# Four of a kernel's first loads on ScalarE's DMA queue, issued after a memset by GpSimd

## The chip, the cores and the metric

The kernel runs on one core of a Trainium2 chip. The metric is device microseconds for one execution, as the median of several runs; less is better. The core has five engines with a queue of instructions each: TensorE (PE), VectorE (DVE), ScalarE (ACT), GpSimd (POOL) and SyncE (SP). SP and ScalarE can also issue transfers between the chip's memory and SBUF. Each of the two has a ring of its own on the same 16 DMA engines; in the rows q1 is SP's ring and q10 is ScalarE's.

## The reference

A gated linear attention (4 batches, 8 heads, 768 steps, head size 48), and a soft mixture of 8 experts with 4 slots each on its output:

```python
f = 1.0 / (1.0 + np.exp(-f_logit))
for t in range(S):
    state = f[:, :, t, :, None] * state + np.einsum('bhd,bhe->bhde', k[:, :, t], v[:, :, t])
    y[:, :, t] = np.einsum('bhd,bhde->bhe', q[:, :, t], state)
...
logits = x @ phi                       # x: (3072, 384), the attention's output
d = softmax of logits over the rows; slot_input = d.T @ x
slot_out[e] = np.maximum(slot_input[e] @ w1[e], 0.0) @ w2[e]
return (softmax of logits over the slots) @ slot_out
```

All inputs and outputs are float32.

## The kernel before, in words

The attention is done in chunks of 128 steps, as 12 blocks u; a block holds half of the heads and batches in tiles of 128 partitions by 1024 columns for f, k and q, and 768 for v. Blocks 0 and 1 are worked off in two halves h of 512 columns, so that the first work can begin after a small load. A step is named as in `load.k.0.1`: the load of k, block 0, half 1. One half load is 128 rows of 2 KB, 256 KB.

For a block, ScalarE takes exp and ln of the gate logits (`d_exp` L267, `d_ln` L271), VectorE runs a prefix sum over them (`d_scan` L274), ScalarE takes exp of it with both signs (`d_g` L277, `d_p` L280), and k and q are multiplied by these (`d_k` L284, `d_q` L288). TensorE transposes k (`kt` L302), forms the scores (L331), which VectorE masks (`s_mask` L336), and then the products with v: `kv` (L348) for the running state, `intra` (L384) and `inter` (L378) for the output. `warm` (L240) is a matmul on constants at the start. The logits, the slot inputs and the two expert layers follow; their weights w1 and w2 are loaded by SP all the while and used in the last third.

The order of all steps is written out by hand in the list `ORDER`, and `keep_order` binds the instructions of each engine to it. `load` (L260) puts a transfer on ScalarE's queue if its name stands in `BY_ACT`, and on SP's otherwise. f has two buffers, and so have k and q.

At the start ScalarE's queue issues k.0.0 and q.0.0, SP's queue f.0.0, f.0.1, f.1.1, q.0.1, f.1.0, k.0.1, v.0 and then the next blocks. GpSimd clears `esum` (`c_esum`, L234: 128x24, named check in the rows), waits for `ones` from VectorE, and makes the mask and the identity.

Of the kernel before, what the change touches and what calls it, by code (L numbers as in the profile page):

```python
# [42 lines left out]
load_phi d_q.1.1 d_ln.2.0 kt.1.0 intra.0.0 d_pend.1 state_t.0 intra.0.1 kt_copy.1 d_scan.2.0 d_ln.2.1 load.f.3 y_copy.0 d_scan.2.1 scores.1.0 d_g.2.0
d_k.2.0 scores.1.1 x_tr.0 s_mask.1.0 d_g.2.1 d_p.2.0 load.q.2 kv.1 load_w2.4 intra.1.0 s_mask.1.1 d_p.2.1 d_k.2.1 d_exp.3 state_t.1 d_ln.3 d_pend.2
hint.Pool d_q.2 kt.2.1 d_scan.3 kt.2.0 intra.1.1 kt_copy.2 x_copy.0 load.v.2 y_copy.1 d_g.3 scores.2.0 scores.2.1 load.q.3 s_mask.2.0 load.k.3 x_tr.1
d_p.3 s_mask.2.1 inter.2 kv.2 load.f.4 intra.2.0 x_copy.1 d_k.3 intra.2.1 kt.3.1 load.k.4 kt.3.0 d_exp.4 load.v.3 d_ln.4 state_t.2 kt_copy.3 d_q.3
load.q.4 d_pend.3 c_lg.0 scores.3.0 d_scan.4 y_copy.2 c_lt.0 load.f.5 scores.3.1 s_mask.3.0 c_max.0 d_g.4 inter.3 d_p.4 kv.3 d_k.4 intra.3.0 c_exp.0
load_w1.4 s_mask.3.1 load_w1.2 hint.SP load.k.5 intra.3.1 c_tr.0.1 load.v.4 c_tr.0.0 d_exp.5 d_q.4 d_pend.4 d_ln.5 kt.4.0 state_t.3 load.f.6 load.q.5
c_copy.0 kt.4.1 x_tr.2 state_s.2 y_copy.3 scores.4.0 kt_copy.4 scores.4.1 d_scan.5 state_s.3 s_mask.4.0 x_copy.2 d_g.5 s_mask.4.1 inter.4 d_exp.6
c_pin.0 c_join.0 d_p.5 d_k.5 d_q.5 c_same.1 kv.4 intra.4.0 d_ln.6 load.v.5 kt.5.1 load_w1.10 x_tr.3 kt.5.0 intra.4.1 x_copy.3 state_t.4 kt_copy.5  # L50
c_lg.1 d_pend.5 load.k.6 load.f.7 y_copy.4 d_scan.6 c_al.0 d_g.6 c_max.1 d_p.6 scores.5.0 scores.5.1 s_mask.5.0 load.q.6 inter.5 c_exp.1 c_lt.1 d_k.6
s_mask.5.1 c_same.3 intra.5.0 load_w1.6 intra.5.1 d_pend.6 load_w2.1 d_q.6 load.v.6 d_exp.7 c_al.1 kt.6.0 load.k.7 kt.6.1 y_copy.5 c_tr.1.0 c_tr.1.1
c_copy.1 kv.5 load.q.7 load.f.8 d_ln.7 kt_copy.6 state_t.5 state_s.4 load_w2.5 x_tr.4 scores.6.0 load.v.7 d_scan.7 s_mask.6.0 scores.6.1 load_w1.3
x_copy.4 inter.6 c_pin.1 d_g.7 intra.6.0 s_mask.6.1 d_k.7 d_exp.8 d_p.7 kv.6 c_join.1 load.q.8 x_tr.5 state_s.5 kt.7.1 d_q.7 state_t.6 kt.7.0
intra.6.1 d_ln.8 load.k.8 load.f.9 x_copy.5 c_sum.1 d_pend.7 c_lg.2 kt_copy.7 d_scan.8 y_copy.6 d_g.8 d_k.8 scores.7.0 scores.7.1 c_max.2 s_mask.7.0
load_w1.1 load.v.8 c_exp.2 c_lt.2 inter.7 load_w1.8 c_tr.2.0 d_p.8 c_tr.2.1 s_mask.7.1 d_exp.9 d_ln.9 intra.7.0 c_copy.2 kv.7 kt.8.1 x_tr.6 load.q.9
state_t.7 kt.8.0 intra.7.1 d_q.8 d_pend.8 load.k.9 x_copy.6 c_soft.0.0 c_sum.0 c_same.0 c_pin.2 c_al.2 d_scan.9 kt_copy.8 c_join.2 state_s.6 y_copy.7
c_soft.1.0 load.f.10 scores.8.1 d_g.9 scores.8.0 c_sum.2 load_w1.0 x_tr.7 d_k.9 d_p.9 x_copy.7 d_pend.9 s_mask.8.0 inter.8 intra.8.0 c_lg.3 d_exp.10
s_mask.8.1 d_ln.10 d_q.9 state_s.7 load_w1.13 kt.9.0 c_lt.3 c_max.3 kt.9.1 load.k.10 kv.8 d_scan.10 load.f.11 load.v.9 c_exp.3 load.q.10 load_w1.12
kt_copy.9 intra.8.1 state_t.8 load.v.10 y_copy.8 c_tr.3.1 d_g.10 c_tr.3.0 d_k.10 scores.9.1 c_al.3 scores.9.0 c_copy.3 state_s.0 x_tr.8 s_mask.9.0  # L60
d_p.10 hint.ACT d_exp.11 load.k.11 s_mask.9.1 c_soft.2.0 load_w1.14 inter.9 x_copy.8 d_ln.11 d_q.10 c_sum.3 d_pend.10 intra.9.0 kv.9 intra.9.1
state_t.9 d_scan.11 state_s.8 load.q.11 load.v.11 c_pin.3 scores.10.1 scores.10.0 y_copy.9 d_g.11 state_s.9 c_join.3 x_tr.9 x_copy.9 s_mask.10.1
d_k.11 inter.10 d_p.11 d_pend.11 s_mask.10.0 c_lg.4 intra.10.0 load_w2.2 intra.10.1 c_max.4 c_exp.4 c_lt.4 d_q.11 c_same.2 load_w1.11 c_tr.4.1
c_tr.4.0 c_copy.4 scores.11.0 y_copy.10 s_mask.11.0 scores.11.1 x_tr.10 c_pin.4 x_copy.10 c_al.4 c_soft.3.0 s_mask.11.1 c_join.4 inter.11 intra.11.0
load_w1.15 load_w2.9 intra.11.1 y_copy.11.0 y_copy.11.1.True end c_lg.5 load_w1.7 flag.0 c_soft.4.0 load_w2.8 x_tr1.11.0 x_tr1.11.1 c_sum.4 c_max.5
c_min.5 c_lt.5 c_exp.5 load_w1.9 load_w1.5 t_max.0 x_copies.11.0 c_tr.5.1 x_copies.11.1 c_tr.5.0 t_max.1 load_w2.10 c_ct.0.0 t_max.2 c_copy.5
load_w2.6 flag.1 c_al.5 c_pre.5 load_w2.14 t_max.3 hint.DVE c_ct.0.1 t_max.4 c_pin.5.0 c_pin.5.1 t_max.5 c_be.5 c_join.5.0 t_psi.0 load_w2.0
c_join.5.1 t_psi.1 load_w2.12 t_psi.2 flag.2 up.0.0.0 up.0.1.0 c_soft.0.1 up.0.0.1 up.0.0.2 load_w2.3 relu.0.0 load_w2.11 up.0.1.1 up.0.1.2 turn.0.0.0
up.1.0.0 turn.0.0.1 relu.0.1 up.1.0.1 down.1.0.0 down.1.0.1 down.0.0.0 down.1.0.2 down.1.0.3 read_flag.Pool down.0.0.1 c_soft.1.1 c_soft.2.1
down.0.0.2 load_w2.16 down.0.0.3 read_flag.ACT up.1.0.2 c_sum.5 up.1.1.0 load_w2.13 c_soft.3.1 relu.1.0 up.1.1.1 turn.0.1.0 t_z.0 turn.1.0.0  # L70
load_w2.15 turn.0.1.1 load_w2.22 up.1.1.2 load_w2.19 down.1.0.4 down.1.0.5 down.1.0.6 turn.1.0.1 down.0.0.4 down.0.0.5 load_w2.7 down.0.0.6 down.0.0.7
c_soft.4.1 down.0.1.0 down.0.1.1 load_w2.17 load_w2.18 relu.1.1 load_w2.21 turn.1.1.0 turn.1.1.1 t_z.1 t_z.2 down.0.1.2 down.1.0.7 down.0.1.3
down.1.1.0 down.0.1.4 down.0.1.5 down.0.1.6 down.0.1.7 down.1.1.1 c_ct.1.0 slot_out.0 slot_out2.0.0 slot_out2.0.1 down.1.1.2 down.1.1.3 c_ct.1.1
combine.0.0 result.0.0.1 result.0.0.3 down.2.0.0 result.0.0.0 combine.0.1 result.0.1.3 down.1.1.4 down.1.1.5 result.0.0.2 down.1.1.6 down.1.1.7
hint.PE down.2.0.1 down.2.0.2 down.2.0.3 load_w2.20 down.2.0.4 result.0.1.2 state_s.1 down.2.0.5 result.0.1.1 load_w2.23 down.2.0.6 result.0.1.0
slot_out.1 slot_out2.1.0 slot_out2.1.1 down.2.0.7 down.2.1.0 down.2.1.1 combine.1.0 down.2.1.2 result.1.0.2 result.1.0.0 down.2.1.3 down.2.1.4
result.1.0.1 down.2.1.5 down.2.1.6 down.2.1.7 combine.1.1 slot_out.2 result.1.0.3 result.1.1.0 result.1.1.1 result.1.1.3 store.0.0 store.0.1
result.1.1.2 slot_out2.2.0 store.1.0 read_flag.PE slot_out2.2.1 combine.2.0 read_flag.DVE result.2.0.0 result.2.0.1 result.2.0.3 store.1.1 combine.2.1
# [898 lines left out]
```

## Time and profile before

| | |
|---|---|
| median of 3 runs | 154.32 us (154.18 to 154.73) |
| the profiled execution | 154.26 us |
| its span, first to last instruction | 152.5 us |
| mean granted TensorE clock | 0.99 |
| TensorE busy | 139.0 us, 91% |
| VectorE busy | 109.2 us, 72% |
| ScalarE busy | 95.2 us, 62% |
| GpSimd busy | 43.7 us, 29% |
| moved by DMA | 53.96 MB, mean 354 GB/s |

The profile is of one execution. Its page lists the busy time of each engine, the chain of work that ended last, and groups of instructions by line. The trace behind it also answers for single stretches: the timeline, the chain in time order, the DMA issues with their time to landing, the packets of each ring, and busy times by window. Times are microseconds from the span's start. SPq and ACTq are the DMA issues of SP and ScalarE. An instruction may start a little before the one ahead of it on its engine has ended. In the rows k, q, f and v all lie in one tile, arena.

### The profile page before, as it was taken

How to read it: one execution, taken by the hardware profiler on the slowest of the kernel's cores; microseconds unless marked ns; L12 is line 12 of the kernel's file. 1: busy time of each engine (PE TensorE's matmuls, PEld its weight loads, DVE VectorE, ACT ScalarE, POOL GpSimd, SP SyncE). 2: the span in 40 equal slices, each digit the busy share in tenths (PEclk: the TensorE clock that was granted, in tenths of full speed). 3: DMA queues.
4: the chain of work that ended last, by engine and by line, in shares of the span. 5: the costliest groups of instructions: out<-in, count | busy, mean ns of one | idle time of the engine just before them, and what ended most of it. 6: DMA issues, size and time to landing. Idle time of an engine off the chain costs nothing.

```text
span 152.5 us, 5621 instructions
## 1 busy us (share of the span) xinstructions
PE 139.0 (91%) x2443; PEld 105.8 (69%) x2443; DVE 109.2 (72%) x155; ACT 95.2 (62%) x160; POOL 43.7 (29%) x50
## 2 busy tenths in 40 slices
...
GB/s 154 333 410 272 292 389 335 275 289 413 401 408 354 360 410 411 404 385 408 312 421 385 385 380 370 401 416 417 408 407 408 410 408 409 247 129 296 258 396 184
DMA packets 14574, 53.96 MB, mean 354 GB/s; under 512 B 1616, under 2 KB 1744, under 8 KB 14544
## 3 DMA queue, kind: packets, MB, share of 16 engines
...
q10 hardware_dynamic: 288, 0.52, 0.9%
q8 instruction: 20, 0.33, 0.8%
q14 instruction: 10, 0.08, 0.2%
...
## 4 chain that ended last, share of the span: by engine, by line
PE 78%; DVE 10%; DMA 4%; ACT 3%; issue 2%; DVEq 0%; SPq 0%; ACTq 0%
PE Y L384 13%; PE T L331 13%; PE Z L616 7%; PE Z L560 7%; PE T L405 6%; PE Y L378 6%; PE T L302 5%; PE T L348 5%; PE T L426 3%; PE Z L641 3%; DVE arena L274 3%; DMA arena<-in_f_dram 2%; DMA out_dram<-wr 2%; PE T L487 2%; DVE arena L336 2%
## 5 line engine op out<-in xcount | busy, mean ns | idle before, releaser
L284 POOL TENSOR_TENSOR arena<-arena 128x1024 f32<-128x1024 f32 (+1 forms) x12 | 25.3, 2111 | 43.4 <-ACT arena L277 37.9
L336 DVE TENSOR_TENSOR arena<-T,mask 128x1024 f32<-128x1024 f32 x24 | 28.3, 1212 | 3.2 <-PE T L331 3.2
L274 DVE TENSOR_TENSOR_SCAN arena<-smask,arena 128x1024 f32<-128x1024 f32 (+1 forms) x15 | 27.8, 1857 | 2.9 <-ACT arena L271 2.2
L331 PEld LDWEIGHTS T<-arena 48*128 48x128 f32 x384 | 22.4, 188 | 4.3 <-issue 2.7
L331 PE MATMUL T<-arena 48*128 48x128 f32 x384 | 24.9, 279 | 0.0
L384 PE MATMUL Y<-arena 128*48 128x128 f32 x368 | 24.5, 275 | 0.0
L384 PEld LDWEIGHTS Y<-arena 128*48 128x48 f32 x368 | 20.1, 123 | 2.4 <-issue 1.7
L288 DVE TENSOR_TENSOR arena<-arena 128x1024 f32<-128x1024 f32 (+1 forms) x14 | 17.1, 1230 | 1.4 <-ACT arena L280 1.3
L394 ACT COPY arena<-Y 112x1024 f32<-112x1024 f32 (+1 forms) x12 | 11.7, 978 | 6.7 <-PE Y L384 4.1
L277 ACT ACTIVATE arena<-arena 128x1024 f32<-128x1024 f32 (+1 forms) x15 | 13.3, 889 | 3.9 <-DVE arena L274 3.6
L662 POOL COPY small<-wr 128x1 f32<-128x1 f32 x1 | 0.2, 189 | 52.6 <-DVE wr L658 52.6
L267 ACT ACTIVATE arena<-arena 128x1024 f32<-128x1024 f32 (+1 forms) x15 | 13.2, 881 | 2.9 <-DMA arena<-in_f_dram 2.9
L271 ACT ACTIVATE arena<-arena 128x1024 f32<-128x1024 f32 (+1 forms) x15 | 13.3, 884 | 0.3
L280 ACT ACTIVATE arena<-arena 128x1024 f32<-128x1024 f32 (+1 forms) x15 | 13.1, 884 | 0.4
L360 POOL TENSOR_TENSOR arena<-arena,check 128x384 f32<-128x384 f32 x8 | 11.5, 1441 | 1.8 <-DVE arena L356 1.8
L408 ACT COPY arena<-T 128x768 f32<-128x768 f32 x11 | 8.7, 795 | 5.1 <-PE T L405 4.5
L302 PE MATMUL T<-ident,arena 112*128 112x112 f32 x80 | 10.5, 266 | 1.4 <-DVE arena L284 1.0
L560 PE MATMUL Z<-wr,lt 128*32 128x512 f32 x96 | 11.1, 595 | 0.4 <-DVE lt L549 0.4
L378 PE MATMUL Y<-arena 48*48 48x128 f32 x304 | 11.1, 274 | 0.0
L405 PE MATMUL T<-ident,arena 112*128 112x112 f32 x88 | 10.7, 264 | 0.3 <-DVE pin L494 0.3
L645 DVE COPY wr<-Z 128x384 f32<-128x384 f32 x12 | 6.0, 552 | 6.9 <-PE Z L641 6.9
L568 DVE TENSOR_TENSOR arena<-Z,emask 128x512 f32<-128x512 f32 x4 | 2.7, 690 | 11.2 <-PE Z L571 11.2
...
## 6 DMA issues: line engine op xcount, KB each, us to landing
...
```

The source lines that it names most:

```text
L271: nc.scalar.activation(x, x, AF.Ln, bias=1.0)
L274: nc.vector.tensor_tensor_scan(cols(R("g"), h), cols(smask, h), cols(R("f", u), h), 0.0, op0=ALU.mult, op1=ALU.add)
L277: nc.scalar.activation(cols(R("f", u), h), cols(R("g"), h), AF.Exp)
L284: (eng or nc.gpsimd).tensor_tensor(x, x, cols(R("f", u), h), op=ALU.mult)
L288: (eng or nc.vector).tensor_tensor(x, x, cols(R("g"), h), op=ALU.mult)
L302: nc.tensor.transpose(ps.T0[:, w, 128 * p : 128 * p + R2], kq[:R2, 4 * w + p], ident[:R2, :R2])
L331: nc.tensor.matmul(TB(u, w)[:, r, 128 * p : 128 * p + 128], kq[rs, 4 * w + p], qq[rs, 4 * w + p], start=True, stop=True)
L336: nc.vector.tensor_tensor(scv[:, w].rearrange("p r a t -> p (r a) t"), TB(u, w).rearrange("p r (a t) -> p (r a) t", t=L), mask.unsqueeze(1 ...
L378: nc.tensor.matmul(y_at(u, p, r, w), st[rs, 4 * w + p], qq[rs, 4 * w + p], start=w == 0 and p < 2, stop=False, skip_group_check=True)
L384: nc.tensor.matmul(y_at(u, p, r, w), vv[:, 4 * w + p, r], scv[:, w, r, p], start=u < 2 and w == 0 and p < 2, stop=w == 1 and p > 1, skip_g ...
L405: nc.tensor.transpose(TX(u)[:, w, 128 * k : 128 * k + R2], yblock(u, w, k), ident[:R2, :R2])
L560: nc.tensor.matmul(upt(j, hf)[32 * qq : 32 * qq + 32], si[:, c], w1u[2 * qq + j, hf][:, c], start=c == 0, stop=c == 2)
```

## The change

`BY_ACT` gets two more entries, so that ScalarE's queue issues k.0.0, q.0.0, q.0.1 and k.0.1, in this order, all ahead of its first `d_exp`. A new step `c_first` lets GpSimd write zeros to the first 256 columns of the place that k.0.0 is loaded to. It comes directly after `c_esum`; the load of k.0.0 has to wait for it, and the loads behind it on ScalarE's queue with it. SP's queue then holds f.0.0, f.0.1, f.1.1, f.1.0, v.0 and the rest. On VectorE and TensorE the order stays as it was; `c_smask` is only written at another place of the list.

```diff
-BY_ACT = (("k", 0, 0), ("q", 0, 0))
+BY_ACT = (("k", 0, 0), ("q", 0, 0), ("q", 0, 1), ("k", 0, 1))
...
 ORDER = """
-c_smask load.f.0.0 c_esum load.f.0.1 load.k.0.0 load.q.0.0 d_exp.0.0 c_ones c_zero warm load.f.1.1 d_ln.0.0 load.q.0.1 load.f.1.0 load.k.0.1 d_exp.0.1
-d_scan.0.0 d_ln.0.1 d_g.0.0 warm d_scan.0.1 c_mask c_ident d_p.0.0 d_g.0.1 warm d_p.0.1 load.v.0 d_exp.1.1 load.k.1 d_pend.0 d_k.0.0 warm d_ln.1.1
+c_esum c_first load.f.0.0 load.f.0.1 load.k.0.0 load.q.0.0 load.q.0.1 load.k.0.1 c_smask d_exp.0.0 c_ones c_zero warm load.f.1.1 d_ln.0.0 load.f.1.0
+d_exp.0.1 d_scan.0.0 d_ln.0.1 d_g.0.0 warm d_scan.0.1 c_mask c_ident d_p.0.0 d_g.0.1 warm d_p.0.1 load.v.0 d_exp.1.1 load.k.1 d_pend.0 d_k.0.0 warm
...
     def c_esum():
         nc.gpsimd.memset(esum, 0.0)
 
+    def c_first():
+
+        nc.gpsimd.memset(cols(R("k", 0), 0)[:, :256], 0.0)
+
...
-    for x, fn in enumerate((c_ones, c_smask, c_ident, c_mask, c_esum, c_zero)):
+    for x, fn in enumerate((c_esum, c_first, c_ones, c_smask, c_ident, c_mask, c_zero)):
```

The rest of `ORDER` is the same list with other line breaks.

## Rows read from the trace of the kernel before

**Rows 1.** The page: TensorE's busy time (part 1), chain by engine (part 4).

```profile
PE 139.0 (91%) x2443; PEld 105.8 (69%) x2443; DVE 109.2 (72%) x155; ACT 95.2 (62%) x160; POOL 43.7 (29%) x50
...
PE 78%; DVE 10%; DMA 4%; ACT 3%; issue 2%; DVEq 0%; SPq 0%; ACTq 0%
```

**Rows 2.** The chain in time order, first 16.5 us: start, duration, what.

```profile
0.81 3.30 DMA arena<-in_f_dram
...
4.20 0.73 ACT arena L267 x2
...
5.58 0.70 ACT arena L267 x2
...
6.96 1.24 DVE arena L274
...
15.09 0.92 PE T L348 x32
```

**Rows 3.** Timeline of VectorE, 8 to 17: start, duration, line, out<-in [idle before].

```profile
9.55 0.69 DVE L288 TENSOR_TENSOR arena<-arena 128x512 f32<-128x512 f32 x1 [0.17 <-ACT arena L280]
10.16 0.68 DVE L284 TENSOR_TENSOR arena<-arena 128x512 f32<-128x512 f32 x1
10.88 2.44 DVE L274 TENSOR_TENSOR_SCAN arena<-smask,arena 128x512 f32<-128x512 f32 x2
```

**Rows 4.** Timeline of all engines: the start, and one later GpSimd memset.

```profile
0.80 0.12 POOL L234 MEMSET check<- 128x24 f32 x1 [0.29 <-POOLq L962]
...
0.81 1.33 SPq L260 DMA_DIRECT2D arena<-in_f_dram  x3
0.83 0.38 ACTq L260 DMA_DIRECT2D arena<-in_k_dram  x1
...
1.25 0.45 ACTq L260 DMA_DIRECT2D arena<-in_q_dram  x1
...
2.18 0.43 SPq L260 DMA_DIRECT2D arena<-in_q_dram  x1
...
2.35 0.29 POOL L231 TENSOR_SCALAR_AFFINE_SELECT mask<-ones 128x128 f32<-128x128 f32 x1 [1.43 <-DVE ones L221]
...
3.13 0.44 SPq L260 DMA_DIRECT2D arena<-in_k_dram  x1
...
4.13 0.33 SPq L260 DMA_DIRECT2D arena<-in_v_dram  x1
...
15.29 0.31 POOL L247 MEMSET emask<- 128x256 f32 x1
```

**Rows 5.** Issue to landing: f.0.0; f.0.1 and f.1.1 (min, max); q.0.1; k.0.1.

```profile
DMA to landing us min/median/max: 3.3/3.3/3.3
...
DMA to landing us min/median/max: 4.3/5.2/6.1
...
DMA to landing us min/median/max: 6.3/6.3/6.3
...
DMA to landing us min/median/max: 6.7/6.7/6.7
```

**Rows 6.** Packets, MB, share of engines by ring: first 2.1 to 2.6, then 2.6 to 3.0.

```profile
q1 hardware_dynamic: 36, 0.07, 42.1%
q10 hardware_dynamic: 12, 0.02, 15.9%
...
q10 hardware_dynamic: 41, 0.08, 54.3%
q1 hardware_dynamic: 33, 0.07, 43.8%
```

**Rows 7.** Windows: length, each engine's busy us (instructions), PEclk, DMA share, GB/s.

```profile
5.00:6.50 1.50, 1.50 (x4) 0.68 (x3) 0.89 (x1) 1.47 (x4) 0.00 (x0) 1.00 0.91 287
6.50:8.00 1.50, 1.45 (x4) 0.38 (x2) 1.38 (x2) 1.47 (x3) 0.00 (x0) 1.00 1.04 399
8.00:10.00 2.00, 1.08 (x6) 0.65 (x6) 1.83 (x4) 1.91 (x5) 0.42 (x1) 1.00 1.05 404
```

More of the change, by code (lines that the diff above doesn't have):

```diff
@@ L43 @@
[L43 to L78, printed above, removed]
@@ L79 @@
-store.2.0.0 result.2.0.2 result.2.1.0 store.2.0.1 result.2.1.3 result.2.1.2 result.2.1.1 store.2.1.1 store.2.1.0 hold.SP hold.DVE hold.ACT hold.Pool
-hold.PE read_flag.SP
+c_esum c_first load.f.0.0 load.f.0.1 load.k.0.0 load.q.0.0 load.q.0.1 load.k.0.1 c_smask d_exp.0.0 c_ones c_zero warm load.f.1.1 d_ln.0.0 load.f.1.0
+d_exp.0.1 d_scan.0.0 d_ln.0.1 d_g.0.0 warm d_scan.0.1 c_mask c_ident d_p.0.0 d_g.0.1 warm d_p.0.1 load.v.0 d_exp.1.1 load.k.1 d_pend.0 d_k.0.0 warm
+d_ln.1.1 d_exp.1.0 d_q.0.0 d_q.0.1 load.q.1 kt.0.0 d_k.0.1 d_scan.1.1 warm d_ln.1.0 d_g.1.1 d_scan.1.0 scores.0.0 kt.0.1 warm kt_copy.0.1 d_k.1.1
@@ new lines @@
+d_g.1.0 load.f.2 kt_copy.0.0 d_p.1.1 s_mask.0.0 d_p.1.0 scores.0.1 d_k.1.0 s_mask.0.1 kt.1.1 load.v.1 d_q.1.0 load.k.2 d_exp.2.0 kv.0 c_emask
+d_exp.2.1 load_phi d_q.1.1 d_ln.2.0 kt.1.0 intra.0.0 d_pend.1 state_t.0 intra.0.1 kt_copy.1 d_scan.2.0 d_ln.2.1 load.f.3 y_copy.0 d_scan.2.1
+scores.1.0 d_g.2.0 d_k.2.0 scores.1.1 x_tr.0 s_mask.1.0 d_g.2.1 d_p.2.0 load.q.2 kv.1 load_w2.4 intra.1.0 s_mask.1.1 d_p.2.1 d_k.2.1 d_exp.3 state_t.1
+d_ln.3 d_pend.2 hint.Pool d_q.2 kt.2.1 d_scan.3 kt.2.0 intra.1.1 kt_copy.2 x_copy.0 load.v.2 y_copy.1 d_g.3 scores.2.0 scores.2.1 load.q.3 s_mask.2.0
@@ new lines @@
+load.k.3 x_tr.1 d_p.3 s_mask.2.1 inter.2 kv.2 load.f.4 intra.2.0 x_copy.1 d_k.3 intra.2.1 kt.3.1 load.k.4 kt.3.0 d_exp.4 load.v.3 d_ln.4 state_t.2
+kt_copy.3 d_q.3 load.q.4 d_pend.3 c_lg.0 scores.3.0 d_scan.4 y_copy.2 c_lt.0 load.f.5 scores.3.1 s_mask.3.0 c_max.0 d_g.4 inter.3 d_p.4 kv.3 d_k.4
+intra.3.0 c_exp.0 load_w1.4 s_mask.3.1 load_w1.2 hint.SP load.k.5 intra.3.1 c_tr.0.1 load.v.4 c_tr.0.0 d_exp.5 d_q.4 d_pend.4 d_ln.5 kt.4.0 state_t.3
+load.f.6 load.q.5 c_copy.0 kt.4.1 x_tr.2 state_s.2 y_copy.3 scores.4.0 kt_copy.4 scores.4.1 d_scan.5 state_s.3 s_mask.4.0 x_copy.2 d_g.5 s_mask.4.1
```

33 lines of the change are left out of this document (31 added, 2 removed).

## The prediction, made before the changed kernel was run

> **What bounds the kernel now.** I read the page first: TensorE is busy for 139.0 of 152.5 us, and it holds 78% of the chain that ended last [rows 1]. No wait of TensorE names a transfer, and the 4% that DMA has of the chain are the two ends: the first load of f and the last store. So a change to the first loads can only act through the moment at which TensorE's unbroken work begins. The chain in time order shows that moment: the 32 matmuls of kv.0 at 15.09, and in front of them one string of work that starts with the load of f.0.0 (0.81, on the chain for 3.30 us) and goes through ScalarE from 4.20 to 6.96 and then VectorE [rows 2]. From 15.09 on the chain is TensorE with short pieces of VectorE. I therefore take what the start gains or loses at 15.09 over to the end one for one.
>
> The next view is VectorE's timeline from 9.5 on [rows 3]: d_q.0.1 at 9.55 waits for ScalarE, and from there d_k.0.1 (10.16) and the scans (10.88) stand end to end. In this stretch a late input of any one of them moves everything behind it.
>
> Last come the transfers: when the eight half loads of block 0 and 1 are issued [rows 4], how long they take to land [rows 5], how the two rings share the engines [rows 6], and what the engines moved [rows 7].
>
> **The change part by part.** *The memset.* c_first is 128x256 on GpSimd, directly behind c_esum (start 0.80, 0.12 us). A memset of that shape took 0.31 [rows 4]. That makes its end 1.23, and with a hop of about 0.05 the first load of ScalarE's queue is issued at 1.28 instead of 0.83: a hold of 0.45 us. If the memset took no longer than the small one, the hold would be 0.25. GpSimd's next operation waits for VectorE until 2.35 [rows 4], so the memset itself costs nothing; with no such wait it would cost 0.31.
>
> *What queues behind the hold.* On ScalarE the four issues k.0.0, q.0.0, q.0.1, k.0.1 and then d_exp.0.0. At 0.45 each, as the issue of q.0.0 took, they run from 1.28 to 3.1, well before f.0.0 lands, so d_exp.0.0 does not wait for them. On SP two issues of 0.43 and 0.44 go away [rows 4], and f.1.0 and v.0 no longer stand behind q.0.1 and k.0.1. v.0 is issued at 4.13, just as f.0.0 lands (0.81 + 3.3 = 4.11) [rows 4, 5], and I expect it to follow that landing again.
>
> *f.0.0 lands earlier.* Between 2.6 and 3.0 the two rings together use 98% of the engines, 41 packets of ScalarE's to 33 of SP's, and between 2.1 and 2.6 ScalarE's moved 12 [rows 6]. These 53 packets are about what the hold takes out of f.0.0's way. At the joint rate of 74 packets in 0.4 us (185 per us) they are worth 53 / 185 = 0.29 us. The ends: 0, if SP's ring by itself went no faster than it does now, as it did between 2.1 and 2.6, where 36 packets left the engines half idle; and 0.45, the whole hold. I take 0.3, since the row with full engines lies nearer to f.0.0's end. d_exp.0.0 then starts at 3.9 instead of 4.20.
>
> *f.0.1 must follow.* It is the second of three issues from 0.81 on, so issued at about 1.22; 4.3 us later is 5.5 [rows 4, 5], and d_exp.0.1 begins at about 5.55 behind ScalarE's own work [rows 2]. There is only 0.05 of cover. But f.0.1 stands behind f.0.0 on the same ring and gets the same head start, so I let it gain the same 0.3. The ends are 0 and 0.45 here too.
>
> *k.0.1 is the cap.* Before, it was issued at 3.13 and landed 6.7 later, at 9.83; d_k.0.1 starts at 10.16 [rows 3 to 5]. From a landing to the start of the work that waits for it passed 0.09 (4.11 to 4.20), so there are 0.24 us of slack and no more: a start that moves by 0.3 finds k.0.1 missing unless it lands earlier too. Now it is the last of four on ScalarE's ring. Two things pull. SP's ring has a lead of 0.45 us, 0.18 MB at 399 GB/s [rows 7]; with equal shares that lead turns up as bytes of v.0 that go ahead of the end of k.0.1, which lands 0.45 later. Against it, between 5.0 and 6.5 the engines moved 287 GB/s and from 6.5 on 399 [rows 7]; in most of that first stretch SP's ring worked alone. If two filled rings close that gap, 1.5 us x 112 GB/s = 0.17 MB come sooner, 0.42 us. I let the two cancel: k.0.1 lands at 9.83 as before, and d_k.0.1 starts at 9.92. The ends of its landing are 9.4 and 10.28.
>
> The Trainium skill (DMA: Bandwidth & Descriptors, Issuing engines are not separate DMA queues) says that loads issued by several engines run on the same 16 engines and interleave, and that a second issuer saves issue time alone. The trace agrees with the interleaving (41 to 33 packets). By that rule the gap would not close, k.0.1 would land at 10.28, and the sum would be a loss of 0.2 us in place of the gain.
>
> *q.0.1* was issued at 2.18 and landed 6.3 later, at 8.48, for d_q.0.1 at 9.55 [rows 3 to 5]: 1.07 of slack, which 0.45 later and a start 0.3 earlier leave positive. f.1.1 landed at about 7.8 (third issue, 6.1 later), and ScalarE does not reach it before d_p.0.1, which d_q.0.1 waits for [rows 3, 5]. Both cost nothing.
>
> **The sum.** The start of d_k.0.1 moves from 10.16 to 9.92, by 0.24. VectorE's string behind it and then TensorE take that along. The profiled execution took 154.26 (span 152.5, 1.8 around it), so it would come to 154.0; the median of the three runs shown is 154.32, 0.06 above, so 154.1. What is late next is k.0.1.
>
> **The rivals.** *k.0.1 comes late: slower than before.* The two rings share equally and SP's lead is filled with v.0. The point from which it decides is a landing after 10.07 (10.16 less 0.09). At 10.28, d_k.0.1 starts at 10.37, 0.2 later than now; if all of v.0 (384 KB, 0.97 us at 404 GB/s [rows 7]) went ahead, it would land at 10.8 and cost 0.73. Time 154.5 to 155.0, the middle 154.65. For it: the nearly equal packet counts [rows 6]. Against: the weak stretch from 5.0 to 6.5, which leaves room [rows 7].
>
> *Everything comes early.* The gap closes, k.0.1 lands at 9.4, and the f loads gain the whole hold of 0.45. Then 154.32 - 0.45 = 153.9. For it: engines full at 2.6 [rows 6]. Against: the last part of f.0.0, after 3.0, still shares.
>
> *The hold does nothing.* SP's ring has its own pace at the start, f.0.0 lands at 4.1 all the same, or the memset is over too early to matter. Then 154.3, provided that k.0.1 is not late. For it: the half idle engines from 2.1 to 2.6. Against: the 98% after it.
>
> **How the numbers follow.** The forecast 154.1 gets 0.42, its own range 153.9 to 154.3. The late k.0.1 gets 0.28, everything early 0.14, the hold without effect 0.11; 0.05 is left for what the trace does not show, such as a later stage that falls otherwise. The range of 153.7 to 154.8 takes in three of the cases and most of the late one, and leaves out its far end and the unnamed rest. 0.5% of this kernel, about what a measurement can tell from no change, is 0.77 us. No named case reaches a gain of that, and only the far end of the late k.0.1 comes near such a loss. So faster 0.06, of the unnamed rest and of sizes misjudged; slower 0.10; same 0.84.
>
> **What would show it.** In the changed profile: ScalarE's first issue at about 1.28; ScalarE's idle time before d_exp.0.0 ending at 3.9; d_k.0.1 at 9.9 with a wait for the load of k in front of it, where before there was none; kv.0 at about 14.85. If d_k.0.1 stands after 10.16 with that wait, the late k.0.1 is right; if it stands there without a wait and d_exp.0.0 at 4.2, the hold did nothing. The prediction is wrong as a whole if kv.0 comes earlier or later and the end does not follow.

## The result and the profile after

| | before | after |
|---|---|---|
| median of 20 runs each | 154.31 us (154.18 to 154.73) | 155.18 us (154.21 to 156.04) |
| ratio to before | | 1.0051, 95% interval 1.0034 to 1.0069 |
| the profiled execution | 154.26 us, span 152.5 | 156.04 us, span 154.3 |
| k.0.1 lands / d_k.0.1 starts | 9.81 / 10.16 | 11.07 / 11.09 |
| first matmul of kv.0 | 15.09 | 15.81 |

The change costs 0.87 us by the medians. The prediction said 154.1 us and no measurable difference, so it was wrong in the sign and outside its range. The profiled execution of after happens to be the slowest of its twenty; four further executions of the same kernel stand below, and what is said of the size of the loss rests on all five. An execution over 1.5% above the fastest of its kernel is left out of the medians, ranges and ratios of this document; there is one, of e13, at 158.06 us.

The page of after: TensorE's busy time, and the chain by engine (for before: [rows 1]).

```profile
PE 140.3 (91%) x2443; PEld 106.3 (69%) x2443; DVE 109.7 (71%) x155; ACT 95.0 (62%) x160; POOL 44.9 (29%) x51
...
PE 47%; DVE 19%; ACT 17%; DMA 8%; issue 5%; POOL 2%; ACTq 0%; SPq 0%; DVEq 0%
```

TensorE does the same work, but its share of the chain fell from 78% to 47%: from kv.0 on the chain of after does not stay in TensorE's own queue, but leaves it for other engines and for transfers in the middle of the kernel as well. Its beginning, in time order (start, duration, what; before: [rows 2]):

```profile
0.81 2.66 DMA arena<-in_f_dram
3.46 0.02 issue
3.48 0.34 ACTq L264
3.82 0.05 issue
3.87 0.73 ACT arena L271 x2
...
15.81 0.93 PE T L352 x32
```

Between the landing of f.0.0 and d_exp.0.0 there now stands an issue of ScalarE, 0.34 us long and started 0.02 after the landing. The timeline of all engines names it (line numbers of after are 4 higher than those of before; before: [rows 3, 4]):

```profile
0.80 0.12 POOL L234 MEMSET check<- 128x24 f32 x1 [0.29 <-POOLq L966]
...
0.81 1.81 SPq L264 DMA_DIRECT2D arena<-in_f_dram  x4
0.85 0.31 POOL L238 MEMSET arena<- 128x256 f32 x1
...
1.19 0.40 ACTq L264 DMA_DIRECT2D arena<-in_k_dram  x1
1.62 0.93 ACTq L264 DMA_DIRECT2D arena<-in_q_dram  x2
...
2.66 0.43 SPq L264 DMA_DIRECT2D arena<-in_v_dram  x1
...
3.48 0.34 ACTq L264 DMA_DIRECT2D arena<-in_k_dram  x1
3.87 0.63 ACT L271 ACTIVATE arena<-arena 128x512 f32<-128x512 f32 x1 [1.78 <-DMA arena<-in_f_dram]
...
9.14 0.69 DVE L292 TENSOR_TENSOR arena<-arena 128x512 f32<-128x512 f32 x1 [0.17 <-ACT arena L284]
...
11.09 0.69 DVE L288 TENSOR_TENSOR arena<-arena 128x512 f32<-128x512 f32 x1 [1.26 <-DMA arena<-in_k_dram]
11.70 2.33 DVE L278 TENSOR_TENSOR_SCAN arena<-smask,arena 128x512 f32<-128x512 f32 x2
```

Read from the top: the memset and the hold are as planned. ScalarE has issued q.0.1 at 2.55 and then issues nothing for 0.93 us; v.0 goes out on SP's queue at 2.66, and k.0.1 only at 3.48, just after f.0.0 has landed (0.81 + 2.66 = 3.47). At the end stands what that does: d_q.0.1 starts 0.41 earlier than before (9.14 against 9.55), and then VectorE stands idle for 1.26 us until k.0.1 is there.

The cause lies in the program. The loads have eight completion semaphores, dealt out in turn when the program is built; the ninth load takes over that of the first, f.0.0, and its issue waits until f.0.0 has landed. In before the ninth is v.0, and k.0.1 is among the first eight. In after v.0 comes ahead of k.0.1 in that deal, although `ORDER` names k.0.1 first, and k.0.1 is the ninth. The traces record for each issue the number of its semaphore and of the one that it waits for: f.0.0 has 101 in both kernels, and so have v.0 in before and k.0.1 in after, which wait for 101. The tenth load (k.1 in both) waits in the same way for f.0.1's, 102, and leaves at 5.54 and 4.96, with f.0.1 landing at 5.53 and 4.94. The waits of SP in before, from 0 to 8 us, show these two issues (us in all, times, the longest):

```profile
SPq L260 <- DMA arena<-in_f_dram: 1.6, 2, 1.1
```

A mere limit of eight loads under way would not do this: in before k.0.0 had landed at 4.30, and k.1 still waited until 5.54. The rows of the kernels below bear it out: the ninth load, and no other, leaves on f.0.0's landing.

| kernel | ninth load | its issue | f.0.0 lands |
|---|---|---|---|
| before | v.0 (SP) | 4.13 | 4.11 |
| after | k.0.1 (ScalarE) | 3.48 | 3.46 |
| e2, move without hold | k.0.1 (ScalarE) | 4.13 | 4.11 |
| e6, before with k.0.1 behind v.0 | k.0.1 (SP) | 4.07 | 4.05 |
| e7, k.0.1 back on SP | v.0 (SP) | 3.48 | 3.47 |

What the late issue meets on the rings, from the DMA view of after: first the issues of v.0 and k.0.1 (KB each, us to landing), then packets, MB and share of the engines by ring from 2.6 to 3.0, the total and the rings from 5 to 8, and the rings from 8 to 10.5 (before: [rows 5 to 7]).

```profile
arena<-in_v_dram SPq DMA_DIRECT2D x1, 384.0 KB, 7.9
...
arena<-in_k_dram ACTq DMA_DIRECT2D x1, 256.0 KB, 7.6
...
q1 hardware_dynamic: 72, 0.12, 81.6%
q10 hardware_dynamic: 16, 0.03, 25.4%
...
DMA packets 539, 1.05 MB, mean 350 GB/s; under 512 B 59, under 2 KB 59, under 8 KB 539
...
q1 hardware_dynamic: 329, 0.68, 65.6%
q10 hardware_dynamic: 210, 0.37, 35.2%
...
q1 hardware_dynamic: 252, 0.83, 81.7%
q10 hardware_dynamic: 125, 0.22, 23.2%
```

From 2.6 to 3.0 SP's ring has 72 packets (0.12 MB) where it had 33 (0.07 MB): this is f.0.0's gain. The last pair is k.0.1's loss. From 8 to 10.5 ScalarE's ring, which then holds little else than k.0.1, moves 0.22 MB, and SP's with v.0 and k.1 0.83 MB. A packet of SP's ring was 3.3 KB there (0.83 MB by 252), one of ScalarE's 1.8 KB; and from 9 on ScalarE's ring has few packets left, 37 until 10.5, against 159 of SP's. So k.0.1 lands 1.26 later than in before: 0.35 by the issue (3.48 against 3.13), 0.9 by the transfer (7.6 against 6.7). The pace of the engines is not the reason. From 5 to 8 they moved 350 GB/s; before it was 343 (the mean of 287 and 399 in [rows 7]). What grew is the amount that goes before k.0.1 is down: from 0 to its landing, first in after (0 to 11.07), then in before (0 to 9.81), the two rings together started

```profile
DMA packets 1517, 3.33 MB, mean 301 GB/s; under 512 B 159, under 2 KB 159, under 8 KB 1517
...
DMA packets 1356, 2.74 MB, mean 280 GB/s; under 512 B 143, under 2 KB 143, under 8 KB 1356
```

At 9.81 after stood at 2.81 MB, no less than before; the other 0.52 MB take 1.24 us at the 420 GB/s of the stretch from 8 to 10.5.

The rest of the loss in this execution is in the middle. d_k.3 on GpSimd, after:

```profile
29.58 2.38 POOL L288 TENSOR_TENSOR arena<-arena 128x1024 f32<-128x1024 f32 x1 [6.08 <-DMA arena<-in_k_dram]
...
31.01 2.03 DVE L292 TENSOR_TENSOR arena<-arena 128x1024 f32<-128x1024 f32 x1
```

and before:

```profile
27.56 2.38 POOL L284 TENSOR_TENSOR arena<-arena 128x1024 f32<-128x1024 f32 x1 [4.78 <-ACT arena L277]
...
30.29 1.22 DVE L288 TENSOR_TENSOR arena<-arena 128x1024 f32<-128x1024 f32 x1
```

In before d_k.3 waits for ScalarE (k.3 has landed just before, at 27.40), and is over when VectorE begins d_q.3, which takes 1.22 us. In after it waits for the load of k.3, which lands at 29.42, starts 2 us later, lies beside d_q.3, and d_q.3 takes 2.03. TensorE, 0.72 behind before since kv.0, is 0.94 behind at 41 us, and 1.50 at 58. The chain in time order shows the way to the second step:

```profile
44.32 2.38 POOL arena L288
...
46.72 0.33 SPq L264
...
47.15 6.96 DMA arena<-in_q_dram
...
56.37 1.36 DVE arena L292
...
58.65 0.99 PE T L409 x8
```

The issue at 46.72 is a load of f into the buffer that this d_k on GpSimd has read, so it waits for the d_k; the load of q behind it on SP's queue goes out at 47.15, 0.93 later than in before, and takes 6.96 us, where it took 6.35. A d_q on VectorE, and then TensorE, come late by that. A last step of 0.28 follows at 122. In this execution the start holds 0.72 of the loss of 1.77, and the way 1.05.

### The profile page after: what moved, and what is told of

The parts are those of the page before. It is cut to its first block, busy times and chain, and to the rows that moved or that the text cites. A ratio compares the mean times of both kernels' runs of the same rounds, so it can differ in the third digit from the quotient of the medians.

```text
span 154.3 us, 5621 instructions
## 1 busy us (share of the span) xinstructions
PE 140.3 (91%) x2443; PEld 106.3 (69%) x2443; DVE 109.7 (71%) x155; ACT 95.0 (62%) x160; POOL 44.9 (29%) x51
## 3 DMA queue, kind: packets, MB, share of 16 engines
q10 hardware_dynamic: 576, 1.05, 1.9%
## 4 chain that ended last, share of the span: by engine, by line
PE 47%; DVE 19%; ACT 17%; DMA 8%; issue 5%; POOL 2%; ACTq 0%; SPq 0%; DVEq 0%
DVE arena L278 8%; PE Z L620 7%; PE Z L564 7%; PE Y L388 6%; PE T L335 5%; DMA arena<-in_q_dram 5%; ACT arena L271 4%; DVE arena L292 4%; ACT arena L275 4%; ACT arena L281 4%; PE T L409 4%; PE Z L645 3%; PE Y L382 2%; ACT arena L284 2%; PE T L352 2%
## 5 line engine op out<-in xcount | busy, mean ns | idle before, releaser
L292 DVE TENSOR_TENSOR arena<-arena 128x1024 f32<-128x1024 f32 (+1 forms) x14 | 18.2, 1303 | 3.4 <-ACT arena L284 3.4
L306 PE MATMUL T<-ident,arena 112*128 112x112 f32 x80 | 10.5, 266 | 1.5 <-DVE arena L288 0.8
L382 PE MATMUL Y<-arena 48*48 48x128 f32 x304 | 11.1, 274 | 0.0
L364 POOL TENSOR_TENSOR arena<-arena,check 128x384 f32<-128x384 f32 x8 | 10.5, 1318 | 1.8 <-DVE arena L360 1.8
```

Source lines behind the costliest of these rows:

```text
L292: (eng or nc.vector).tensor_tensor(x, x, cols(R("g"), h), op=ALU.mult)
```

## The experiments

Three theories on the start were tested first. A: the loss is k.0.1, which lands too late. B: the hold does it, since all loads of ScalarE's queue begin later. C: f.0.1 is delayed by the loads that share the engines with it. Each time is a median with its range, and the ratio is to runs of before on the same chip in the same job, with its 95% interval.

### Each half of the change alone: e1 and e2

e1 has the memset and the queues of before, e2 the queues of after and no memset.

```diff
 # e1, against after
-BY_ACT = (("k", 0, 0), ("q", 0, 0), ("q", 0, 1), ("k", 0, 1))
+BY_ACT = (("k", 0, 0), ("q", 0, 0))
 # and load.q.0.1, load.k.0.1 in ORDER where before has them
 # e2, against after
-c_esum c_first load.f.0.0 load.f.0.1
+c_esum load.f.0.0 load.f.0.1
```

> The memset and the wait stay, but ScalarE's queue has k.0.0 and q.0.0 alone; q.0.1 and k.0.1 are back on SP's ring, ahead of v.0, in the order of the kernel before. Theory A (the loss is the late k.0.1 on ScalarE's ring): f.0.0 lands at about 3.5, d_exp.0.0 starts at 3.55 to 3.6, k.0.1 lands at 9.5 to 9.9, d_k.0.1 starts at 9.6 to 9.95 and kv.0 at 14.5 to 14.9 (before 15.09, changed kernel 15.81); the time is 153.7 to 154.1. Theory B (holding the first loads is itself the loss): d_k.0.1 and kv.0 are late as in the changed kernel, kv.0 at 15.5 or later, time 154.9 to 155.3.

> Four loads on ScalarE's queue, without the memset. k.0.1 still waits for the landing of f.0.0 before it is issued, and v.0 is still ahead of it on SP's ring. Theory A (late k.0.1): f.0.0 lands at 4.1 again, k.0.1 is issued at about 4.1 and lands later than 11.07, d_k.0.1 starts at 11.2 to 11.9, kv.0 at 15.9 to 16.6, time 155.1 to 156. Theory B (the hold is the loss): d_k.0.1 at about 10.2, time 154.2 to 154.5.

e1: 154.41 us (153.85 to 155.04, 12 runs), ratio 1.0002 (0.9982 to 1.0021). e2: 155.04 us (154.37 to 156.45, 12 runs), ratio 1.0052 (1.0028 to 1.0076). A loss of the same size is there without the memset, and none of it with the memset alone, so B falls. VectorE's timeline of e1:

```profile
9.36 0.69 DVE L292 TENSOR_TENSOR arena<-arena 128x512 f32<-128x512 f32 x1 [0.65 <-DMA arena<-in_q_dram]
10.63 0.69 DVE L288 TENSOR_TENSOR arena<-arena 128x512 f32<-128x512 f32 x1 [0.58 <-DMA arena<-in_k_dram]
```

and of e2:

```profile
7.69 1.22 DVE L278 TENSOR_TENSOR_SCAN arena<-smask,arena 128x512 f32<-128x512 f32 x1 [0.54 <-ACT arena L275]
...
10.88 0.68 DVE L288 TENSOR_TENSOR arena<-arena 128x512 f32<-128x512 f32 x1
```

With the hold alone f.0.0 lands at 3.35 (before: 4.11), so the hold does what it is for; but VectorE then waits for q.0.1 and k.0.1, and nothing is left of it. I had expected k.0.1 at 9.5 to 9.9; on SP's ring and issued at 3.13 as in before, it landed at 10.61. So the hold, too, can make it late, and by 9.81 the rings had started 2.59 MB there against 2.74 in before; why is not shown. With the move alone f.0.0 lands at 4.11 as in before, and f.0.1 at 6.25 instead of 5.53: the scan waits for ScalarE, and d_k.0.1 is late without a wait of its own. k.0.1, issued at 4.13, landed at 10.72, so d_k.0.1 (10.88) could not have started before that in any case: in e2 A alone would cost some 0.58 of the 0.72 by which kv.0 is late. The late f.0.1 is C, and it is seen where loads of ScalarE's queue go out unheld or, in e3, with no ninth among them; in the five traces of after f.0.1 landed at 4.94 to 5.10 (5.37 in e5), earlier than in before.

### k.0.1 among the first eight again, on ScalarE's queue: e3

A small memset by GpSimd on v.0's place, late enough that v.0 becomes the ninth load again.

```diff
+def c_vfirst():
+    nc.gpsimd.memset(R("v", 0)[:, :64], 0.0)
 # in ORDER directly behind c_ident
```

> The changed kernel, and v.0 held behind a second small memset of GpSimd (end about 3.3). By that k.0.1 becomes the eighth load issued and v.0 the ninth: k.0.1 no longer waits for the landing of f.0.0 and is issued at about 2.55 instead of 3.48, and v.0 at about 3.5 instead of 2.66. Theory A (late k.0.1, by that wait and by v.0 ahead of it): k.0.1 lands at 9.6 to 10.3 instead of 11.07, d_exp.0.0 starts at 3.55 instead of 3.87, d_k.0.1 starts at 9.7 to 10.4, kv.0 at 14.6 to 15.3, time 153.8 to 154.6. Theory B (ScalarE's ring as such is slow, or the hold): k.0.1 lands at 10.8 or later again, time 154.9 to 155.3.

155.04 us (154.17 to 155.6, 12 runs), ratio 1.0044 (1.0025 to 1.0063): the gain that I expected did not come. k.0.1 was issued at 2.58 and landed at 10.05, and v.0 went out at 3.39 behind f.0.0 (3.31). But f.0.1 landed at 5.88:

```profile
7.31 1.22 DVE L281 TENSOR_TENSOR_SCAN arena<-smask,arena 128x512 f32<-128x512 f32 x1 [1.34 <-ACT arena L278]
...
10.51 0.68 DVE L291 TENSOR_TENSOR arena<-arena 128x512 f32<-128x512 f32 x1
```

The scan waits 1.34 us for ScalarE, which waited for f.0.1; d_k.0.1 has no wait and is 0.35 later than in before. So the fourth load in a row on ScalarE's ring costs f.0.1 what k.0.1 gains, as far as one trace shows (with three in a row f.0.1 landed at 4.94 in after and 4.97 in e7). To move both loads lost either way: with k.0.1 held it is late itself, without that it makes f.0.1 late.

### What a delay at this place costs: e4 and e13

Both put a memset on VectorE in front of d_k.0.1, with nothing else changed about it: e4 in before (128x1024), e13 in after (128x2048, long enough to hide k.0.1's landing). They give the price of a delay that is sure.

```diff
+def c_delay():
+    nc.vector.memset(R("sc")[:, :1024], 0.0)      # e13: all of sc
-kt.0.0 d_k.0.1 d_scan.1.1
+kt.0.0 c_delay d_k.0.1 d_scan.1.1
```

> The kernel before, with one more memset of VectorE (128x1024 of zeros, some 0.9 us by the one of smask) right ahead of d_k.0.1; no load is moved. d_k.0.1 starts at about 11.05 as in the changed kernel. If what is lost at the start goes to the end one for one and nothing more is lost: kv.0 at 15.9 to 16.0, time 155.1 to 155.25, runs as close together as before (within 0.6). If lateness alone makes later loads late and costs more: time above 155.5, or runs spread over 1.5 us and more as in the changed kernel. If there is slack later that takes it up: 154.3 to 154.8.

e4: 155.09 us (154.93 to 155.67, 7 runs), ratio 1.0056 (1.0035 to 1.0077). VectorE's timeline:

```profile
10.49 0.91 DVE L237 MEMSET arena<- 128x1024 f32 x1 [0.16 <-DVE arena L291]
11.32 0.63 DVE L287 TENSOR_TENSOR arena<-arena 128x512 f32<-128x512 f32 x1
```

kv.0 stands at 15.96, 0.87 later, and 0.0056 of 154.3 is 0.86: by the ratio a delay of d_k.0.1 reaches the end one for one. Five of the seven runs lie within 0.16 us, while those of after spread over 1.8 and those of e2 over 2.1. The other two, 155.59 and 155.67, are half a us slower, and the trace is of the slowest: its span is 1.40 longer than that of before, and TensorE, 0.87 behind at kv.0, is 1.33 behind at 58. So the steps between 53 and 58 that the profiled execution of after shows come with a late start in some executions even where no load was moved. Before itself spread over 1.2 us in the 30 runs beside e4.

> The changed kernel with a memset of VectorE of 128x2048 (some 1.8 us) ahead of d_k.0.1, so that d_k.0.1 starts at about 11.75 however late k.0.1 lands; kv.0 is then at about 16.4, 1.3 us later than before, in every run. Theory A (all of the loss, and the spread of the runs, comes in through the time at which k.0.1 lands): the time is that of the kernel before plus 1.3 us, 155.5 to 155.8, and the runs lie as close together as with the delay in the kernel before (most within 0.3 us). Theory F (the changed loads lose some 0.3 us more on the way, past the start): 155.9 or more, or runs spread over more than 1.2 us.

e13: 156.00 us (155.71 to 156.02, 4 runs), ratio 1.0096 (1.0079 to 1.0113). Its one trace is of the execution of 158.06 us: TensorE's granted clock was 1.00 from 10 to 13, where it was busy for 1.48 us, 0.56 from 13 to 16, and 0.50, the lower of its two levels (1.2 GHz), from 16 to 19. So only VectorE's start is read:

```profile
11.94 0.63 DVE L291 TENSOR_TENSOR arena<-arena 128x512 f32<-128x512 f32 x1
...
14.72 0.67 DVE L291 TENSOR_TENSOR arena<-arena 128x512 f32<-128x512 f32 x1
```

k.0.1 landed at 9.96 here, well ahead of 11.94. The second row is d_k.1.1, which was at 13.24 in before: a shift of 1.48 us, where I had counted with 1.3. 0.0096 of 154.5 is 1.48, give or take 0.27. By the ranges that I had set, the time is that of theory F and the spread, 0.3 us in four runs, that of A; with the start as it was, 1.48 late, nothing of the time is left for F. This speaks for A and against a loss in the changed queues themselves further on, but it rests on four runs and one start.

### Slack in front of d_k.0.1: e5

```diff
 # in ORDER of after
-kt.0.0 d_k.0.1 d_scan.1.1
+kt.0.0 d_scan.1.1 d_k.0.1
```

> The changed kernel with one swap on VectorE: d_scan.1.1 goes ahead of d_k.0.1, which gives k.0.1 some 1.3 us more before it is needed; no load is touched. Theory A (in most runs the loss is k.0.1 landing late): VectorE runs the scan from about 10.4 to 11.6 while k.0.1 is on its way, d_k.0.1 follows without a wait, kv.0 starts at 15.1 to 15.3 instead of 15.81, time 154.4 to 154.7. Theory C (in most runs the loss is f.0.1 landing late, because ScalarE's ring with more loads in it shares with SP's; k.0.1 is only second): the swap helps nothing, time 155.0 to 155.3.

154.92 us (154.24 to 155.45, 12 runs), ratio 1.0037 (1.0019 to 1.0055), less back than I expected.

```profile
10.72 1.23 DVE L278 TENSOR_TENSOR_SCAN arena<-smask,arena 128x512 f32<-128x512 f32 x1 [0.64 <-ACT arena L275]
11.86 0.67 DVE L288 TENSOR_TENSOR arena<-arena 128x512 f32<-128x512 f32 x1
```

k.0.1 landed at 11.09, and no wait for it is left. The scan that was pulled ahead waits 0.64 us for ScalarE instead, whose d_ln.1.1 runs from 10.00 to 10.63, and d_k.0.1 stands still later, at 11.86. The wait changed its name, and kv.0 came at 15.62.

### k.0.1 as the ninth, on SP's queue: e6

```diff
 # in ORDER of before; v.0 leaves its place behind d_p.0.1
-load.f.1.0 load.k.0.1 d_exp.0.1
+load.f.1.0 load.v.0 load.k.0.1 d_exp.0.1
```

> The kernel before, with v.0 issued ahead of k.0.1 on SP's ring and nothing else: two loads on ScalarE's queue, no memset. k.0.1 becomes the ninth load, waits for the landing of f.0.0 (4.1) and stands behind v.0. Theory A (late k.0.1): it lands at 10.6 to 11.0 instead of 9.81, d_k.0.1 starts at 10.7 to 11.1, kv.0 at 15.6 to 16.0, time 154.8 to 155.2. Theory C (f.0.1 late through ScalarE's ring): that ring is as before, d_k.0.1 at 10.2 to 10.4, time 154.2 to 154.5.

154.34 us (154.11 to 155.37, 12 runs), ratio 1.0014 (0.9993 to 1.0034), where I expected a clear loss. k.0.1 was issued at 4.07, later than in after, and landed at 10.07:

```profile
10.11 0.68 DVE L284 TENSOR_TENSOR arena<-arena 128x512 f32<-128x512 f32 x1
```

That is just in time. So to be the ninth and behind v.0 does not alone make k.0.1 late. On one ring the loads landed in the order of their issue (v.0 at 9.40, k.0.1 at 10.07, k.1 at 11.35), and up to k.0.1's landing the rings had started 2.90 MB; in after k.0.1 has a ring to itself, SP's ring with v.0 and then k.1 goes on beside it, and it was 3.33 MB.

### Only q.0.1 moved: e7

```diff
-BY_ACT = (("k", 0, 0), ("q", 0, 0), ("q", 0, 1), ("k", 0, 1))
+BY_ACT = (("k", 0, 0), ("q", 0, 0), ("q", 0, 1))
 # and in ORDER load.k.0.1 directly behind load.f.1.0
```

> The changed kernel, with k.0.1 back on SP's ring between f.1.0 and v.0; the memset, and k.0.0, q.0.0 and q.0.1 on ScalarE's queue, stay. k.0.1 is issued at about 2.65 without a wait and has no v.0 ahead of it. Theory A: it lands at 9.7 to 10.4, d_k.0.1 starts at 9.8 to 10.5, kv.0 at 14.7 to 15.4, time 154.0 to 154.6. Theory C: f.0.1 lands after 5.5 in most runs since q.0.1 too shares with it now, time 154.9 to 155.3.

154.22 us (153.59 to 155.6, 12 runs), ratio 0.9988 (0.9961 to 1.0015). With the hold kept and k.0.1 the eighth load, on SP's queue at 2.66, the start is what I had predicted of the change and more: f.0.0 at 3.47, k.0.1 at 9.60, kv.0 at 14.54, 0.55 earlier than in before. VectorE's timeline, its start and the middle:

```profile
9.64 0.69 DVE L288 TENSOR_TENSOR arena<-arena 128x512 f32<-128x512 f32 x1
...
29.75 2.15 DVE L292 TENSOR_TENSOR arena<-arena 128x1024 f32<-128x1024 f32 x1
```

and GpSimd's:

```profile
28.44 2.37 POOL L288 TENSOR_TENSOR arena<-arena 128x1024 f32<-128x1024 f32 x1 [6.21 <-PE Y L382]
```

But of 0.55 us only 0.11 is left in the span (152.43 against 152.54). VectorE is earlier in the middle, k.3 is not (its load was down at 28.28, in before at 27.40), d_k.3 lies beside d_q.3, and that takes 2.15 instead of 1.22. The row puts d_k.3's wait down to TensorE's matmuls of L382, but in after d_k.3 began before these had ended (29.58, they ran to 29.63); in both kernels it began 0.16 after k.3 had landed. After it the gain is 0.21. e7 is the best version that I found, and it can't be told from before; its interval does not rule out the whole 0.55 either.

### The weights in front of k.3: e9, e10 and e11

A new theory, D: the loss in the middle comes from the load of w2.4, which SP's queue issues ahead of k.3. It goes from behind kv.1 to just ahead of load_w1.4, in after (e9), in e7 (e10) and in before (e11).

```diff
-kv.1 load_w2.4 intra.1.0
+kv.1 intra.1.0
-load_w1.4 s_mask.3.1
+load_w2.4 load_w1.4 s_mask.3.1
```

> The changed kernel with one 512 KB load of weights (the first w2) taken out from between the loads of block 2 and put behind those of block 4, some 15 us later; the start is untouched. Theory D (the loss beyond the start is made on the way: k.3 lands late behind the weights, d_k.3 on GpSimd starts later and falls on d_q.3 of VectorE, which then takes 2.0 us instead of 1.2, and TensorE waits around 41 and 55 us): k.3 lands about 1.2 us earlier than in the changed kernel (28.2 or earlier instead of 29.4), d_k.3 starts before 28.8, d_q.3 takes 1.2 us; kv.0 stays at 15.4 to 15.9, and the time comes down to 154.6 to 154.95. Theory E (all of the loss is at the start, the rest is noise): time 155.0 to 155.3 as before.

> The kernel with the memset and three loads on ScalarE's queue (k.0.1 on SP's, ahead of v.0), with the same load of weights moved. There kv.0 had come 0.55 us earlier than before and the end only 0.11. Theory D (the gain of the start was given back on the way by loads that land late): kv.0 at 14.5 to 14.9 and the end now 0.3 to 0.6 earlier than before, time 153.7 to 154.0. Theory E: 154.1 to 154.4, no better.

> The kernel before with the load of weights moved in the same way, as the measure for the two others. Theory D: the kernel before has only its slower runs (154.6 to 155.7) to win; kv.0 at 15.1, median 154.1 to 154.3. If the move is itself a gain or a loss of over 0.3 us, it shows here, and the two others are to be read against it.

e9: 155.34 us (154.94 to 155.96, 6 runs), ratio 1.0069 (1.0054 to 1.0084). e10: 154.55 us (154.01 to 155.56, 12 runs), 1.0015 (0.9995 to 1.0035). e11: 154.74 us (154.36 to 155.9, 7 runs), 1.0037 (1.0015 to 1.0058). In e9 d_q.3 took 1.22 us again, so the first half of D holds. But between 55 and 58 us, where TensorE waits for VectorE's pieces of work, its delay still grew from 0.42 to 0.70, and the time did not fall: at 155.34 it lies above what either theory had expected. In before the move costs 0.57 us by itself, which with a start of 0.42 is about the 1.07 that e9 is late by. As a remedy D falls.

### More executions of after and before: e8, e12, e14, e15 and e16

Both kernels unchanged, one execution each, to see how much k.0.1's landing varies.

> The changed kernel once more, for a second trace, since the one shown is of an execution of 156.04, the slowest of twenty. Theory A: f.0.0 lands at about 3.4, k.0.1 is issued with that landing, lands at 10.4 to 11.0, and d_k.0.1 waits for it (start 10.5 to 11.1), while d_q.0.1 starts before 9.5. Theory C: f.0.1 lands after 5.5 and d_q.0.1 starts after 9.7, with no wait of d_k.0.1 for k.0.1.

> The changed kernel, a third trace. k.0.1 is issued with the landing of f.0.0 at about 3.5 and lands at 10.5 to 11.1; d_k.0.1 waits for it; kv.0 at 15.3 to 15.8. The end is later than before by the same amount, plus 0 to 1 us where d_k.3 falls on d_q.3 (then d_q.3 takes over 1.5 us).

> The changed kernel, a fourth trace: where kv.0 starts and where the end is. Theory A: kv.0 later than before by 0.3 to 0.75 us, as k.0.1 lands, and the end later by the same. Theory F: the end later by 0.2 to 1 us more than kv.0, with loads of blocks 3 to 7 landing over 1 us later than before.

> The changed kernel, a fifth trace, for the same two numbers: the start of kv.0 and the end. Theory A: both are later than before by the same, 0.3 to 0.75 us. Theory F: the end by 0.2 to 1 us more than kv.0.

> The kernel before, a second trace. Theory A: kv.0 at 15.05 to 15.1 again, since k.0.1 has slack there, whatever its landing (8.9 to 9.8); the end as far behind kv.0 as in the first trace, 137.4 us, plus 0 to 1 where loads land late on the way.

d_k.0.1 in VectorE's timeline, of e8:

```profile
10.80 0.69 DVE L288 TENSOR_TENSOR arena<-arena 128x512 f32<-128x512 f32 x1 [0.94 <-DMA arena<-in_k_dram]
```

of e14, and of e15:

```profile
11.40 0.69 DVE L288 TENSOR_TENSOR arena<-arena 128x512 f32<-128x512 f32 x1 [1.06 <-DMA arena<-in_k_dram]
```

```profile
10.62 0.69 DVE L288 TENSOR_TENSOR arena<-arena 128x512 f32<-128x512 f32 x1 [0.66 <-DMA arena<-in_k_dram]
```

| execution | f.0.0 | f.0.1 | k.0.1 | v.0 | kv.0 | span | time |
|---|---|---|---|---|---|---|---|
| before | 4.11 | 5.53 | 9.81 | 10.77 | 15.09 | 152.54 | 154.26 |
| before, e16 | 4.13 | 5.36 | 9.31 | 10.27 | 15.03 | 152.51 | 154.25 |
| after | 3.46 | 4.94 | 11.07 | 10.59 | 15.81 | 154.31 | 156.04 |
| after, e8 | 3.49 | 4.95 | 10.78 | 10.37 | 15.52 | 152.98 | 154.71 |
| after, e12 | 3.49 | 4.99 | 10.90 | 10.41 | 15.63 | 153.26 | 154.99 |
| after, e14 | 3.41 | 4.96 | 11.37 | 11.14 | 16.11 | 153.82 | 155.55 |
| after, e15 | 3.59 | 5.10 | 10.60 | 10.10 | 15.33 | 152.82 | 154.55 |

In all five executions of after k.0.1 lands after v.0, VectorE waits for it, and kv.0 is late by 0.72, 0.43, 0.54, 1.02 and 0.24, on the mean 0.59. The spans are longer by 1.77, 0.44, 0.72, 1.28 and 0.28, on the mean 0.90; the medians say 0.87. So in four of the five the start is nearly all of it (0.01 to 0.26 comes behind it), and the profiled execution with its 1.05 us in the middle is the exception.

All the kernels together, the shift of kv.0 against before's 15.09 in one trace, and the time by the ratio:

| | kv.0 | time by the ratio | what limits the start |
|---|---|---|---|
| e1 | +0.25 | +0.03 (-0.28 to +0.32) | q.0.1 and k.0.1 |
| e2 | +0.72 | +0.80 (+0.43 to +1.17) | f.0.1 |
| e3 | +0.40 | +0.68 (+0.39 to +0.97) | f.0.1 |
| e4 | +0.87 | +0.86 (+0.54 to +1.19) | the memset |
| e5 | +0.53 | +0.57 (+0.29 to +0.85) | d_ln.1.1 |
| after | +0.59, mean of 5 | +0.79 (+0.52 to +1.06) | k.0.1 |
| e13 | +1.48 (d_k.1.1) | +1.48 (+1.22 to +1.75) | the memset |
| e6 | -0.04 | +0.22 (-0.11 to +0.52) | as before |
| e7 | -0.55 | -0.19 (-0.60 to +0.23) | nothing late |
| e9, w2.4 later | +0.42 | +1.07 (+0.83 to +1.30) | k.0.1 |
| e10, w2.4 later | -0.54 | +0.23 (-0.08 to +0.54) | nothing late |
| e11, w2.4 later | -0.03 | +0.57 (+0.23 to +0.90) | as before |

Where nothing but the start was changed, a delay goes through to the end. Of a gain the traces show less there: 0.11 of 0.55 in e7, and 0.26 of 0.54 in e10, which moves w2.4 as well.

## Why the prediction was wrong, point by point

*What bounds the kernel.* Right for delays: kv.0's moment goes to the end one for one (e4, e13). Wrong for gains. "I take what the start gains or loses at 15.09 over to the end one for one" holds upward only, as far as one trace shows: in e7 0.55 us at kv.0 is 0.11 at the end. There k.3 landed no earlier, and with an earlier VectorE that shows, as d_q beside GpSimd's d_k. The chain of before could not show this, since it names only what ended last in that execution.

*The memset.* Right in kind, small in size: it began at 0.85, beside c_esum, and the first load of ScalarE's queue went out at 1.19, not 1.28.

*f.0.0 and f.0.1.* Right in direction, the term was mis-sized: 0.65 us instead of 0.3 (3.46 against 4.11), more even than the end of 0.45, and 0.59 for f.0.1 (4.94 against 5.53). I had counted the packets of ScalarE's ring up to 3.0, "these 53 packets"; f.0.0 shared the engines until it landed at 4.11. e1 and e2 show that all of it is the hold's (3.35 and 4.11).

*"So d_exp.0.0 does not wait for them".* This step failed. It started at 3.87, close to the 3.9 that I wrote, but for another reason: f.0.0 had landed at 3.46, and the issue of k.0.1 stood ahead of d_exp.0.0 on ScalarE and took 0.34. In e7, without that issue, d_exp.0.0 starts at 3.49. It cost nothing at the end, since VectorE stood idle for 1.26 us behind it all the same.

*"v.0 is issued at 4.13, just as f.0.0 lands, and I expect it to follow that landing again".* This is the step on which the rest hangs. I saw the coincidence in [rows 4, 5], took it for something that belongs to v.0, and did not ask what makes a load wait for another load's landing. It belongs to the ninth load. Had I asked, the move would have shown its own price: v.0 free at 2.66, k.0.1 bound to f.0.0.

*"I let the two cancel: k.0.1 lands at 9.83 as before".* Failed: 10.60 to 11.37 in five executions, all outside the ends 9.4 and 10.28 (with the same loads 11.09 in e5 and 10.78 in e9; 9.96 in e13). SP's lead was not 0.45 us but 0.82 (2.66 to 3.48), and all of v.0 and a part of the loads behind it went ahead: 3.33 MB up to k.0.1's landing against 2.74. The weak stretch was not filled: 350 GB/s from 5 to 8 against 343. The Trainium skill (DMA: Bandwidth & Descriptors, Issuing engines are not separate DMA queues) has loads of several engines interleave on the same 16 and grants a second issuer only its issue time; by that rule the gap would not close, and the trace agrees. The term that was mis-sized is this lead: I had counted with 0.18 MB more ahead of k.0.1, and it was 0.59.

*The slack.* The 0.24 us in front of d_k.0.1 came from one trace. In the kernels that leave the loads up to k.0.1 as they were (before, e16, e4, e11) it landed at 9.81, 9.31, 8.96 and 8.94, while kv.0 of before and e16 moved by 0.06. 9.81 is thus the late end of a spread of 0.9 us, which the slack covers in before and which nothing covers in after.

*The rivals.* "k.0.1 comes late" is what happened, by its far end: "if all of v.0 went ahead, it would land at 10.8 and cost 0.73". The landings of after lie around that, and the loss is 0.87. I gave this rival 0.28 but left its far end out of the range, since nothing that I had read let all of v.0 go ahead. The agreement is partly luck: the rival has equal shares and a lead of 0.45 us, and did not see the late issue at 3.48.

What stays open: why a load like k.3 lands 1 to 2 us later in some executions than in others (in e16, of before, 0.75 later, with 1.53 for d_q.3 and the same span), and so how the 0.3 us of the mean that is lost behind kv.0 divides between the start and chance (e13 says that nothing clear is lost there with a fixed start, e4's trace loses 0.53 there with no load moved, and e9 was not better than after); how much of k.0.1's lateness is the late issue, how much the loads that go ahead and how much the hold, which e1, e3 and e6 do not separate; and why e11 costs 0.57 us in its runs, when its one trace has kv.0 at 15.06 and a span of 152.51.
